# Attention scores on padded keys, a shorter way to the scale of the values, and output products that begin at the last transpose

## The chip, the cores and the metric

The kernel runs on one core of a Trainium2 chip. The metric is the device time of one execution in microseconds (us); of several runs the median is given. The profile is that of one execution.

## What is computed

The program is a chain of three layers in float32. The first is attention with rotary positions, for 4 batches, 8 heads, 576 positions and 64 features per head; two feed-forward layers follow, on 576 positions of 512 features.

```python
q_rot, k_rot = (rotate(q), rotate(k))
scores = scale * np.matmul(q_rot, k_rot.transpose(0, 1, 3, 2))
scores = scores - np.max(scores, axis=-1, keepdims=True)
attn = np.exp(scores)
attn = attn / (np.sum(attn, axis=-1, keepdims=True) + 1e-09)
return np.matmul(attn, v).astype(np.float32)
...
k = np.maximum(xk @ w_k, 0.0)
v = k * k @ w_v
r = 1.0 / (1.0 + np.exp(-(xr @ w_r)))
return (r * v).astype(np.float32)
...
h = np.maximum(xt @ w_tok1, 0.0) @ w_tok2
u = x + h.transpose(0, 2, 1)
h2 = np.maximum(u @ w_ch1, 0.0) @ w_ch2
return (u + h2).astype(np.float32)
```

## The kernel before

Every float32 product is made of three (high by high, high by low, low by high), with operands split into two parts that TensorE takes in one pass each.

Heads are worked on in 16 pairs, `g`, four for each batch. The rotated queries and keys of a pair lie in SBUF tiles of 128 rows, 64 features of the first head above 64 of the second, as a high and a low part: `spl_t[g]` holds `(kh, kl), (qh, ql)`, all of them `kq` in the rows of the profile. A pair has nine blocks of scores, `r` = 0 to 8, each of 128 query rows by 576 keys: eight are four blocks for each of the two heads, `m` the block and `x` the head, and the ninth holds the last 64 rows of both heads. `emit_S` (L366) makes a block with six matmuls into `S`, which has three PSUM buffers. A block of one head reads 64 rows of the tiles, `l`; the ninth block reads all 128, since its queries are padded with zeros. TensorE is then used in another shape: 64\*128 in the profile's rows, against 128\*128. `r` runs through the heads in turn: 0, 1, 0, 1.

VectorE takes the largest of each row (`emit_max`), ScalarE the exponentials (`emit_exp`), VectorE the reciprocals (`emit_rc`); ScalarE and VectorE make two halves in float16 (`emit_hi`, `emit_lo`). Then a transfer issued by SyncE (SP) transposes them (`emit_tr`, L415) into `pt` tiles, one for each head and each half `u` of the query rows. `emit_pv` (L426) makes the output of one half `u` of both heads, with 28 matmuls of 128\*64, the two heads in turn on the two halves of the array's columns.

The values are scaled by a power of two for each pair. `v_max` takes the largest of each row, `v_row` (L310) lays the 128 results side by side in one row by a product with the identity, `v_pow` finds the power on that row, `v_all` (L331) spreads it over 128 rows by a product with a row of ones, and `v_sc` (L337) copies it to SBUF. `v_shift` moves rows of the scaled values by transfers from SBUF to SBUF.

`a_step(j, kv)` (L492) writes the steps of all blocks; `prep(g, k)` (L453) writes the loads and the preparation of the next pairs between them. In batch 0 the weights of the second layer are prepared beside it (`Conv`). From batch 1 on, `kv` weaves the products `kp` and `vp` of the second layer, with 128\*128 matmuls, between the blocks (`kvr_gen`). The order on each engine is not that of the code alone: the framework's scheduler sorts the instructions by priorities (`PRI`, the `prio` decorators) and by times that it assumes. All transfers go through SP's one queue, in its order. The rest of the program, after 475 us, is the other two layers.

Of the kernel before, what the change touches and what calls it, by code (L numbers as in the profile page):

```python
# [8 lines left out]
F32 = mybir.dt.float32  # L9
# [9 lines left out]
NP = H // 2  # L19
# [45 lines left out]
def body(tc, kin, qin, vw, tabs, ident, mu, w_k, w_v, w_r, w_t1, w_t2, w_c1, w_c2, out):  # L65
# [41 lines left out]
    with ctx:  # L107
# [3 lines left out]
        vd = [[dram.tile([128, KD, HS], F32, name=f"vd{b}_{c}") for c in range(2)] for b in range(B)]  # L111

        idn = const.tile([128, 128], F32, name="idn")
        ones = const.tile([1, 128], F32, name="ones")
        mu_s = const.tile([128, 2, KD], F32, name="mu_s")
        om_s = const.tile([128, 2, KD], F32, name="om_s")

# [120 lines left out]
        rk_p = right("rk", BUFS["rk"])  # L238
        rq_p = right("rq", BUFS["rq"])
        tab_p = right("tab", 1)  # L240
        sp_p = right("sp", BUFS["sp"])
        vr_p = right("vr", BUFS["vr"])
        v16_p = right("v16", BUFS["v16"])
# [5 lines left out]

        tab = tab_p.tile([128, 2, QW], F32, name="tab")  # L250
        TAB = [[tab[:, k, 0:w] for k in range(2)] for w in (S, QW)]

        raw_t, v_t, v16_t, sc_t, spl_t = {}, {}, {}, {}, {}
        NG = B * NP
# [23 lines left out]
        def rope(g, j, k, e, lo=0, hi=None):  # L278
# [6 lines left out]
            if e == "P":  # L285
                last["rope"] = o

        @prio("qk")
        def split_hi(g, j, e, lo=0, hi=None):
            w = QW if j else S  # L290
            if lo == 0:
                hl = [sp_p.tile([128, w], F32R, tag=f"sp{j}{i}", name="kq") for i in range(2)]
                spl_t.setdefault(g, [None, None])[j] = hl
            hi = hi or w
            copy(e, spl_t[g][j][0][:, lo:hi], raw_t[g][j][0][:, lo:hi])

        @prio("qk")
        def split_lo(g, j, e, lo=0, hi=None):
            hi = hi or (QW if j else S)
            hl = [x[:, lo:hi] for x in spl_t[g][j]]  # L300
            tt(e, hl[1], raw_t[g][j][0][:, lo:hi], hl[0].bitcast(F32), ALU.subtract)

        @prio("v")
        def v_max(g):
            m = sm_p.tile([128, 1], F32, tag="vm", name="vm")
            dve.tensor_reduce(out=m, in_=v_t[g], op=ALU.max, axis=AX.XY, apply_absolute_value=True)
            sc_t[g] = m

        @prio("v")
        def v_row(g):  # L310
            p = pv_p.tile([128, 512], F32, tag="pv", name="vps")
            pe.matmul(p[0:1, 0:128], lhsT=sc_t[g], rhs=idn, start=True, stop=True)
            sc_t[g] = p

        @prio("v")
        def v_pow(g):

            p = sc_t[g]
            a = sm_p.tile([1, 2], F32, tag="va", name="va")
            dve.tensor_reduce(out=a[:, 0:1], in_=p[0:1, 0:128], op=ALU.max, axis=AX.X)  # L320
            dve.tensor_scalar(out=a[:, 0:1].bitcast(I32), in0=a[:, 0:1].bitcast(I32), scalar1=0x7F800000,
                              scalar2=None, op0=ALU.bitwise_and)
            r = sm_p.tile([1, 2], F32, tag="vb", name="vb")
            dve.tensor_scalar(out=a[:, 1:2], in0=a[:, 0:1], scalar1=2.0 ** -100, scalar2=2.0 ** -14,
                              op0=ALU.max, op1=ALU.mult)
            dve.tensor_scalar(out=r[:, 1:2], in0=a[:, 1:2], scalar1=1.0 / PSCALE, scalar2=None, op0=ALU.mult)
            dve.reciprocal(r[:, 0:1], a[:, 1:2])
            sc_t[g] = r

        @prio("v")  # L330
        def v_all(g):  # L331
            p = pv_p.tile([128, 512], F32, tag="pv", name="vps2")
            pe.matmul(p[:, 0:2], lhsT=ones, rhs=sc_t[g], start=True, stop=True)
            sc_t[g] = p

        @prio("v")
        def v_sc(g):  # L337
            s = sc_p.tile([128, 2], F32, tag="sc", name="sc")
            dve.tensor_copy(s, sc_t[g][:, 0:2])
            sc_t[g] = s  # L340

        @prio("v16")
        def v_hi(g):
# [18 lines left out]
        S_t, sum_t, p16_t = {}, {}, {}  # L362
        pt_t, xT = {}, {}

        @prio("S")
        def emit_S(j):  # L366
            g, r = divmod(j, ND)
            (kh, kl), (qh, ql) = spl_t[g]
            m, x = divmod(r, 2)
            l = slice(0, 128) if r == ND - 1 else slice(64 * x, 64 * x + 64)  # L370
            p = S_t[j] = S_p.tile([128, 2, 512], F32, tag="S", name="S")
            for h in range(2):
                for n, (a, b) in enumerate(((qh, kh), (qh, kl), (ql, kh))):
                    pe.matmul(p[:, h, 0:HS], lhsT=a[l, 128 * m:128 * m + 128], rhs=b[l, h * HS:(h + 1) * HS],  # L374
                              start=(n == 0), stop=(n == 2))
# [38 lines left out]
        @prio("tr")  # L414
        def emit_tr(j):  # L415
            g, r = divmod(j, ND)
            m, x = divmod(r, 2)
            t = p16_t[j].rearrange("p a b c -> p (a b c)")
            if r == ND - 1:
                for y in range(2):  # L420
                    sp.dma_start_transpose(out=pt(g, y, 1)[:, :, 256:320], in_=t[64 * y:64 * y + 64])
            else:
                sp.dma_start_transpose(out=pt(g, x, m // 2)[:, :, 128 * (m % 2):128 * (m % 2) + 128], in_=t)

        @prio("pv")
        def emit_pv(g, u):  # L426

            t0, n = UNIT[u]
            ts = [pt_t.pop((g, x, u)) for x in range(2)]
            vh, vl = v16_t[g]  # L430
            p = pv_p.tile([128, 512], F32, tag="pv", name="pv")
            prods = [(vh, j, j) for j in range(9)] + [(vl, j, j) for j in range(5)]
            for i, (v, a, c) in enumerate(prods):
                for x in range(2):
                    l = slice(64 * x, 64 * x + 64)
                    pe.matmul(p[l, 0:n], lhsT=v[:, a, l], rhs=ts[x][:, c, :], start=(i == 0),  # L436
                              stop=(i == len(prods) - 1))

            @prio("low")
            def out():  # L440
                b, pr = divmod(g, NP)
                if b not in xT:
                    xT[b] = P["xT"].tile([128, KD, S + 1], F32, tag="xT", name="xT")
                    pool.memset(xT[b][:, :, 0:1], 0.0)
                copy("D", xT[b][:, pr, 1 + t0:1 + t0 + n], p[:, 0:n], sc_t[g][:, 1:2])
                if u == 1:
                    sp.dma_start(xd[b][:, pr], xT[b][:, pr])
                    a_done.add(g)
            return out
# [3 lines left out]
        def prep(g, k):  # L453
# [12 lines left out]
                split_hi(g, 0, "A")  # L466
                v_pow(g)
            elif k == 1:
                v_all(g)
                v_sc(g)  # L470
                ld_raw(g + 1, 0, 0)
                ld_raw(g + 1, 0, 1)
            elif k == 2:
# [5 lines left out]
            elif k == 4:  # L479
                split_hi(g, 1, "A")  # L480
                split_lo(g, 1, "D")
                v_hi(g)
            elif k == 5:
                v_lo(g)
                v_shift(g)
            elif k == 6:
                v_max(g + 1) if g + 1 < NG else None

        NTT = NG * ND
        after = {}  # L490
# [174 lines left out]


        n0 = UNIT[0][1]
        usual, PRI["ld"] = PRI["ld"], 0
        ld_raw(0, 0, 0)
        sp.dma_start(tab[:, 0], tabs[:, 0])  # L670
# [10 lines left out]
        for j in range(2):  # L681
            for k in range(2):
                ld_raw(1, j, k)
        pool.memset(ones, 1.0)
        cv = Conv(lambda: P["xs"].tile([128, 2 * HS], I32, tag="xs", name="cv"),
                  wk + wv, "conv0", "rope", "P", lambda: acc_p.tile([128, 512], I32, tag="acc", name="cvp"))
        for j in range(2):
# [13 lines left out]
        v_max(0)  # L701
        v_row(0)
        v_pow(0)
        v_all(0)
        v_sc(0)
        v_hi(0)
        v_lo(0)
        v_shift(0)
# [298 lines left out]
```

## Time and profile before

| | us |
|---|---|
| median of 3 runs | 1004.59 (1001.96 to 1006.24) |
| profiled execution, span from the first to the last instruction | 997.5 |
| TensorE (PE) busy in that span | 900.2 |
| its weight loads (PEld) | 822.1 |
| VectorE (DVE) | 584.9 |
| ScalarE (ACT) | 483.7 |
| GpSimd (POOL) | 429.9 |

No other time is listed for the profiled execution than its span; what lies around the span is therefore taken from the median of the runs, 7.1 us above it. Shares of busy time are means over stages that differ: the transfer engines are busy half of the span, and nearly all of that falls into the first half. The matmuls' ends are modelled and overlap, so the distance from one start to the next tells more of TensorE's pace than their durations do. "issue" is a wait for nothing that the profile shows.

### The profile page before, as it was taken

To read this page: it belongs to the slowest core of one execution; us is meant where nothing else is said; L and a number is where in the kernel's file an instruction comes from. 1 tells how busy PE (TensorE), PEld (TensorE's weight loads), DVE (VectorE), ACT (ScalarE), POOL (GpSimd) and SP (SyncE) were. 2 spreads that over 40 slices of the span, in tenths; PEclk is the share of its full clock that TensorE was granted. 3 is DMA by queue.
4 is the path that set the end of the run, shared out by engine and by line. 5 is a ranking of instruction groups with operands and counts; after the bars stand their busy time and mean duration, and the time that the engine had idled before them with its cause. 6 is when DMAs were issued, how large, how long until landed. Compare 5 with 4: busy or idle time off the path is not lost.

```text
span 997.5 us, 17692 instructions
## 1 busy us (share of the span) xinstructions
PE 900.2 (90%) x6544; PEld 822.1 (82%) x6544; DVE 584.9 (59%) x1280; ACT 483.7 (48%) x1077; POOL 429.9 (43%) x445
## 2 busy tenths in 40 slices
PE   2654698999999889999799989999999999999997
PEld 2534466888887778888689979999999999999997
DVE  7989977767777677776897599532133211332111
ACT  3556666767677677675564565421143112211110
POOL 6257967777768765351675522410141013101010
PEclk9966658999999999999999999999999999999999
DMA  5999979898899977786920372110211001000000
GB/s 183 247 259 268 198 145 201 175 189 175 181 175 189 190 149 145 130 160 143 326 94 25 123 290 82 32 42 1 72 37 37 1 25 55 1 24 24 1 25 25
DMA packets 212343, 120.81 MB, mean 121 GB/s; under 512 B 175264, under 2 KB 193312, under 8 KB 212128
## 3 DMA queue, kind: packets, MB, share of 16 engines
q1 hardware_dynamic: 212256, 119.67, 50.9%
q8 instruction: 52, 0.85, 0.3%
q14 instruction: 35, 0.29, 0.1%
HBM read 60.90 MB, written 14.16 MB: 75 GB/s over the span
## 4 chain that ended last, share of the span: by engine, by line
PE 54%; DVE 6%; DMA 2%; POOL 2%; ACT 1%; issue 1%; SPq 0%; DVEq 0%; ACTq 0%; POOLq 0%
PE c1p L545 5%; PE co L545 5%; PE c1p L546 5%; PE c1p L547 5%; PE co L546 5%; PE co L547 5%; PE S L374 3%; PE pv L436 2%; PE rp L545 2%; PE rp L546 2%; PE rp L547 2%; PE vp L545 2%; PE vp L546 1%; PE kp L545 1%; PE vp L547 1%
## 5 line engine op out<-in xcount | busy, mean ns | idle before, releaser
L374 PE MATMUL S<-kq 64*128 64x288 f32 (+1 forms) x864 | 159.8, 342 | 32.2 <-DVE p L406 15.1
L374 PEld LDWEIGHTS S<-kq 64*128 64x128 f32 (+1 forms) x864 | 127.3, 214 | 59.2 <-issue 18.9
L387 ACT ACTIVATE S<-S,nm 128x576 f32<-128x576 f32 x144 | 102.2, 713 | 77.9 <-DVE nm L380 77.3
L906 DVE SCALAR_TENSOR_TENSOR hs<-c1p,hs 128x288 fp32r<-128x288 f32 x96 | 43.6, 454 | 158.0 <-ACT hs L905 157.9
L380 DVE TENSOR_REDUCE nm<-S 128x1 f32<-128x576 f32 x144 | 106.7, 750 | 43.0 <-PE S L374 42.6
L905 ACT ACTIVATE hs<-c1p 128x288 fp32r<-128x288 f32 x96 | 38.9, 409 | 183.8 <-PE c1p L547 180.3
L406 DVE SCALAR_TENSOR_TENSOR p<-S,rc,p 128x576 f16<-128x576 f32 x144 | 114.6, 810 | 16.7 <-ACT p L75 16.1
L104 POOL TENSOR_TENSOR uhl<-y,uhl 128x288 fp32r<-128x288 f32 x32 | 25.4, 822 | 223.9 <-ACT uhl L73 223.9
L545 PE MATMUL c1p<-uhl,parts 128*128 128x288 f32 x384 | 115.0, 300 | 3.6 <-DVE y L104 3.6
L546 PE MATMUL c1p<-uhl,parts 128*128 128x288 f32 x384 | 114.3, 298 | 0.0
L547 PE MATMUL c1p<-uhl,parts 128*128 128x288 f32 x384 | 114.2, 298 | 0.0
L75 ACT ACTIVATE p<-S,rc 128x576 f16<-128x576 f32 x144 | 104.9, 750 | 18.1 <-ACT S L387 7.4
L546 PE MATMUL co<-hs,parts 128*128 128x288 f32 x384 | 112.7, 296 | 0.0
L547 PE MATMUL co<-hs,parts 128*128 128x288 f32 x384 | 112.7, 296 | 0.0
L545 PE MATMUL co<-hs,parts 128*128 128x288 f32 x384 | 108.4, 297 | 0.0
L545 PE MATMUL kp<-xs,parts 128*128 128x288 f32 x256 | 80.9, 323 | 8.6 <-ACT t L614 5.5
L436 PE MATMUL pv<-pt,vh 128*64 128x256 f16 (+1 forms) x576 | 60.8, 328 | 29.8 <-DMA pt<-p 22.6
L545 PE MATMUL vp<-k,parts 128*128 128x288 f32 x256 | 78.7, 310 | 2.3 <-ACT vt L73 1.6
L104 POOL TENSOR_TENSOR q<-t 128x288 f32<-128x288 f32 x64 | 47.8, 749 | 72.9 <-ACT t L614 67.2
L546 PE MATMUL kp<-xs,parts 128*128 128x288 f32 x256 | 77.0, 302 | 0.1
L546 PE MATMUL vp<-k,parts 128*128 128x288 f32 x256 | 77.0, 302 | 0.0
L545 PEld LDWEIGHTS c1p<-uhl,parts 128*128 128x128 f32 x384 | 73.1, 190 | 4.5 <-POOL uhl L104 3.8
(119 smaller groups left out, 2363.1 us busy)
## 6 DMA issues: line engine op xcount, KB each, us to landing
words<-in_w_c_dram SPq DMA_DIRECT2D x24, 512.0 KB, 6.8
rq<-in_qin_dram SPq DMA_DIRECT2D x30, 320.0 KB, 3.6
rk<-in_kin_dram SPq DMA_DIRECT2D x32, 288.0 KB, 3.5
vr<-in_vw_dram SPq DMA_DIRECT2D x16, 320.0 KB, 3.6
xd<-xT SPq DMA_DIRECT2D x16, 288.5 KB, 2.7
vd<-vt SPq DMA_DIRECT2D x32, 144.0 KB, 2.4
y<-vd SPq DMA_DIRECT2D x8, 576.0 KB, 5.5
out_dram<-y SPq DMA_DIRECT2D x8, 576.0 KB, 3.6
```

The lines of the kernel that those rows point to most:

```text
L75: act.activation(out=o, in_=i, func=AF.Copy, scale=scale)
L104: return (pool if e == "P" else dve).tensor_tensor(o, a, b, op=op)
L374: pe.matmul(p[:, h, 0:HS], lhsT=a[l, 128 * m:128 * m + 128], rhs=b[l, h * HS:(h + 1) * HS], start=(n == 0), stop=(n == 2))
L380: dve.tensor_reduce(out=nm, in_=S_t[j][:, :, 0:HS], op=ALU.max, axis=AX.XY, negate=True)
L387: act.activation(out=e, in_=e, func=AF.Exp, bias=sum_t[j], accum_out=s)
L406: dve.scalar_tensor_tensor(out=t[:, 1], in0=S_t.pop(j)[:, :, 0:HS], scalar=sum_t[j], in1=t[:, 0], op0=ALU.mult, op1=ALU.subtract)
L436: pe.matmul(p[l, 0:n], lhsT=v[:, a, l], rhs=ts[x][:, c, :], start=(i == 0), stop=(i == len(prods) - 1))
L545: pe.matmul(p, lhsT=wh, rhs=t[:, 0], start=first, stop=False)
L546: pe.matmul(p, lhsT=wh, rhs=t[:, 1], start=False, stop=False)
L547: pe.matmul(p, lhsT=wl, rhs=t[:, 0], start=False, stop=last)
L905: act.activation(out=h[:, 0], in_=p[:, 0:HS], func=AF.Relu)
L906: dve.scalar_tensor_tensor(out=h[:, 1], in0=p[:, 0:HS], scalar=0.0, in1=h[:, 0].bitcast(F32), op0=ALU.max, op1=ALU.subtract)
```

## The change

Three things change. For batches 1 to 3 the keys of each head are copied by transfers (`apart`, L317 in the new numbering) into tiles `kz` of 128 rows of their own, whose other 64 rows hold zeros from the start (`zeros`); a block's scores are then made with all 128 rows, of which 64 add nothing. There is one such tile for each head and each part, so that a pair's copy follows the last use by the pair before. The blocks' order by head becomes 0, 0, 1, 1 (`place`). In the output products the second head now comes first. And the first product of the values' scale takes the column of maxima, repeated 128 times, as its stationary operand, so that the row of maxima arrives on all 128 rows at once and the second product and the copy fall away.

```diff
+        kz = [[kz_p.tile([128, S], F32R, tag=f"kz{x}{i}", name="kz") for i in range(2)] for x in range(2)]
...
+        def zeros(x):
+
+            for i in range(2):
+                pool.memset(kz[x][i][64 - 64 * x:128 - 64 * x].bitcast(F32), 0.0)
...
+        @prio("qk")
+        def apart(g, x):
+
+            if g < NP:
+                return
+            l = slice(64 * x, 64 * x + 64)
+            for i in range(2):
+                sp.dma_start(kz[x][i][l].bitcast(F32), spl_t[g][0][i][l].bitcast(F32))
...
-            pe.matmul(p[0:1, 0:128], lhsT=sc_t[g], rhs=idn, start=True, stop=True)
+            pe.matmul(p[:, 0:128], lhsT=sc_t[g].broadcast_to([128, 128]), rhs=idn, start=True, stop=True)
...
-        @prio("v")
-        def v_all(g):
-            p = pv_p.tile([128, 512], F32, tag="pv", name="vps2")
-            pe.matmul(p[:, 0:2], lhsT=ones, rhs=sc_t[g], start=True, stop=True)
-            sc_t[g] = p
-
-        @prio("v")
-        def v_sc(g):
-            s = sc_p.tile([128, 2], F32, tag="sc", name="sc")
-            dve.tensor_copy(s, sc_t[g][:, 0:2])
-            sc_t[g] = s
...
+        def place(r):
+
+            return (4, 0) if r == ND - 1 else (2 * (r // 4) + r % 2, r // 2 % 2)
...
-            m, x = divmod(r, 2)
-            l = slice(0, 128) if r == ND - 1 else slice(64 * x, 64 * x + 64)
+            m, x = place(r)
+            l = slice(0, 128)
+            if r < ND - 1 and g >= NP:
+                kh, kl = kz[x]
+            elif r < ND - 1:
+                l = slice(64 * x, 64 * x + 64)
...
-                for x in range(2):
+                for x in (1, 0):
...
+                apart(g, 0)
             elif k == 6:
                 v_max(g + 1) if g + 1 < NG else None
+            elif k == 7:
+                apart(g, 1)
```

The scheduler moves instructions with it. On TensorE, around the first half's output products of the sixth pair (`g` = 5), before (`pv` are output products, `S` scores, `kp` the second layer's):

```order
L374 MATMUL S<-kq 128x288 x12
L436 LDWEIGHTS vh
L436 MATMUL pv<-pt_2014,vh 64x256
L545 MATMUL kp<-xs,parts 128x288
L546 MATMUL kp<-xs,parts 128x288
L547 MATMUL kp<-xs,parts 128x288
...
L436 LDWEIGHTS vh
L436 MATMUL pv<-pt_2075,vh 64x256
```

The same place of the changed kernel:

```order
L386 MATMUL S<-kz,kq 128x288 x6
L448 LDWEIGHTS vh
L448 MATMUL pv<-pt_2135,vh 64x256
L448 LDWEIGHTS vh
L448 MATMUL pv<-pt_2007,vh 64x256
L448 LDWEIGHTS vh
...
L558 MATMUL kp<-xs,parts 128x288
```

Before, one product stands alone ahead of twelve `kp` matmuls and the rest behind them; now all 28 stand together, and the scores read `kz`.

On SP's queue, from the fifth pair's first transposes on (`pt<-p` are transposes, `vh<-vh` the shift of the values), before:

```order
L423 DMA_TRANSPOSE pt_1605<-p_1567 128x9x128
L263 DMA rk<-in_kin_dram 128x576
L266 DMA rq<-in_qin_dram 128x640
L423 DMA_TRANSPOSE pt_1570<-p_1602 128x9x128
L423 DMA_TRANSPOSE pt_1605<-p_1623 128x9x128
L447 DMA xd_60<-xT 128x577
L359 DMA vh<-vh 64x512
L360 DMA vh<-vh 64x512
L274 DMA vr<-in_vw_dram 128x640
L423 DMA_TRANSPOSE pt_1719<-p_1674 128x9x128
L423 DMA_TRANSPOSE pt_1767<-p_1716 128x9x128
L423 DMA_TRANSPOSE pt_1719<-p_1764 128x9x128
```

The changed kernel there:

```order
L435 DMA_TRANSPOSE pt_1643<-p_1591 128x9x128
L459 DMA xd_60<-xT 128x577
L363 DMA vh<-vh 64x512
L364 DMA vh<-vh 64x512
L435 DMA_TRANSPOSE pt_1643<-p_1611 128x9x128
L317 DMA kz<-kq 64x576 x2
L276 DMA vr<-in_vw_dram 128x640
L435 DMA_TRANSPOSE pt_1708<-p_1663 128x9x128
L435 DMA_TRANSPOSE pt_1708<-p_1705 128x9x128
L435 DMA_TRANSPOSE pt_1841<-p_1755 128x9x128
L317 DMA kz<-kq 64x576 x2
```

The two copies of the first head (high and low part) now stand behind the fourth transpose of a pair, and those of the second head behind the seventh, ahead of the eighth.

## Rows read from the trace of the kernel before

**Rows 1.** Busy time by stretch: PE, PEld, DVE, ACT, POOL, clock, DMA share, GB/s.

```profile
25.00:145.00 120.00, 76.95 (x409) 60.23 (x408) 106.27 (x231) 72.46 (x144) 77.78 (x69) 0.68 0.99 231
145.00:475.00 330.00, 313.58 (x2370) 262.58 (x2368) 234.98 (x559) 231.84 (x511) 206.88 (x218) 0.98 0.85 168
```

**Rows 2.** Timeline of TensorE, 168 to 173 us: start, duration (us), instruction.

```profile
168.63 0.30 PE L547 MATMUL kp<-xs,parts 128*128 128x288 f32 x1
168.76 0.96 PE L374 MATMUL S<-kq 128*128 128x288 f32 x6
169.56 0.29 PE L545 MATMUL kp<-xs,parts 128*128 128x288 f32 x1
...
171.03 0.30 PE L547 MATMUL kp<-xs,parts 128*128 128x288 f32 x1
171.26 1.05 PE L374 MATMUL S<-kq 64*128 64x288 f32 x6
172.25 0.40 PE L545 MATMUL kp<-xs,parts 128*128 128x288 f32 x1
172.49 0.29 PE L546 MATMUL kp<-xs,parts 128*128 128x288 f32 x1
```

**Rows 3.** Waits, 150 to 475 us: who waited for whom, total, times, longest.

```profile
PEld L436 <- issue: 12.4, 59, 1.2
PEld S L374 <- issue: 12.1, 59, 1.2
...
PE pv L436 <- DMA pt<-p: 5.5, 8, 1.5
...
PE S L374 <- DVE p L406: 5.3, 6, 1.7
```

**Rows 4.** Timeline of TensorE around an early output product, 189 to 192 us.

```profile
189.53 0.30 PE L436 MATMUL pv<-pt,vh 128*64 128x256 f16 x1
189.76 0.40 PE L545 MATMUL kp<-xs,parts 128*128 128x288 f32 x1
...
191.34 0.30 PE L547 MATMUL kp<-xs,parts 128*128 128x288 f32 x1
191.57 1.17 PE L436 MATMUL pv<-pt,vh 128*64 128x256 f16 x17
```

**Rows 5.** The tile `vps` of the values' scale: durations, and what its engine waited for.

```profile
L333 PEld LDWEIGHTS vps<-vb,ones x32: 181/184/333, 20.3 to 425.3; 1*128 1x128 f32 x32
...
  DVE vb L327: 17.7, 9
```

**Rows 6.** Timeline of TensorE around scores of both heads, 300 to 303 us.

```profile
300.92 0.30 PE L547 MATMUL kp<-xs,parts 128*128 128x288 f32 x1
301.15 1.44 PE L374 MATMUL S<-kq 64*128 64x288 f32 x12
...
302.75 0.29 PE L546 MATMUL kp<-xs,parts 128*128 128x288 f32 x1
```

**Rows 7.** Transposes in 150 to 475 us; the values' shift, issue and landing.

```profile
L423 SPq DMA_TRANSPOSE pt<-p x97: 1242/1305/2971, 149.9 to 473.5; - x97
...
L359 SPq DMA_DIRECT2D vh<-vh x16: 472/487/865, 23.1 to 437.8; - x16
...
DMA to landing us min/median/max: 2.0/2.8/6.0
```

**Rows 8.** Timeline of SP and TensorE at two passages from pair to pair.

```profile
191.47 5.57 SPq L423 DMA_TRANSPOSE pt<-p  x3
...
206.73 1.06 PE L374 MATMUL S<-kq 64*128 64x288 f32 x6
...
335.98 3.78 SPq L423 DMA_TRANSPOSE pt<-p  x2
...
338.85 1.86 PE L374 MATMUL S<-kq 64*128 64x288 f32 x18
```

**Rows 9.** Timeline of GpSimd at the start, 0 to 12 us.

```profile
8.59 2.46 POOL L104 TENSOR_TENSOR rq<-rq,tab 128x384 f32<-128x384 f32 x2 [7.59 <-DMA rq<-in_qin_dram]
```

More of the change, by code (lines that the diff above doesn't have):

```diff
@@ L113, in body @@
         idn = const.tile([128, 128], F32, name="idn")
-        ones = const.tile([1, 128], F32, name="ones")
         mu_s = const.tile([128, 2, KD], F32, name="mu_s")
@@ L240, in body @@
         tab_p = right("tab", 1)
+        kz_p = right("kz", 1)
         sp_p = right("sp", BUFS["sp"])
@@ L318, in v_pow @@
             p = sc_t[g]
-            a = sm_p.tile([1, 2], F32, tag="va", name="va")
-            dve.tensor_reduce(out=a[:, 0:1], in_=p[0:1, 0:128], op=ALU.max, axis=AX.X)
+            a = sm_p.tile([128, 2], F32, tag="va", name="va")
+            dve.tensor_reduce(out=a[:, 0:1], in_=p[:, 0:128], op=ALU.max, axis=AX.X)
             dve.tensor_scalar(out=a[:, 0:1].bitcast(I32), in0=a[:, 0:1].bitcast(I32), scalar1=0x7F800000,
                               scalar2=None, op0=ALU.bitwise_and)
-            r = sm_p.tile([1, 2], F32, tag="vb", name="vb")
+            r = sc_p.tile([128, 2], F32, tag="sc", name="sc")
             dve.tensor_scalar(out=a[:, 1:2], in0=a[:, 0:1], scalar1=2.0 ** -100, scalar2=2.0 ** -14,
                               op0=ALU.max, op1=ALU.mult)
+            dve.reciprocal(r[:, 0:1], a[:, 1:2])
             dve.tensor_scalar(out=r[:, 1:2], in0=a[:, 1:2], scalar1=1.0 / PSCALE, scalar2=None, op0=ALU.mult)
-            dve.reciprocal(r[:, 0:1], a[:, 1:2])
             sc_t[g] = r
-        @prio("v")
-        def v_all(g):
-            p = pv_p.tile([128, 512], F32, tag="pv", name="vps2")
-            pe.matmul(p[:, 0:2], lhsT=ones, rhs=sc_t[g], start=True, stop=True)
-            sc_t[g] = p
-        @prio("v")
-        def v_sc(g):
-            s = sc_p.tile([128, 2], F32, tag="sc", name="sc")
-            dve.tensor_copy(s, sc_t[g][:, 0:2])
-            sc_t[g] = s
         @prio("v16")
@@ L416, in emit_tr @@
             g, r = divmod(j, ND)
-            m, x = divmod(r, 2)
+            m, x = place(r)
             t = p16_t[j].rearrange("p a b c -> p (a b c)")
@@ L468, in prep @@
             elif k == 1:
-                v_all(g)
-                v_sc(g)
                 ld_raw(g + 1, 0, 0)
@@ L667, in body @@
         n0 = UNIT[0][1]
+        zeros(0)
+        zeros(1)
         usual, PRI["ld"] = PRI["ld"], 0
@@ L683, in body @@
                 ld_raw(1, j, k)
-        pool.memset(ones, 1.0)
         cv = Conv(lambda: P["xs"].tile([128, 2 * HS], I32, tag="xs", name="cv"),
@@ L703, in body @@
         v_pow(0)
-        v_all(0)
-        v_sc(0)
         v_hi(0)
@@ L959 @@
     lay = {}
-    z = _np.zeros((B, NP, D, 64), f32)
     def features(x, h):
@@ L965, in features @@
         return x, _np.concatenate([x[..., D // 2:, :], x[..., :D // 2, :]], axis=-2)
+    z = _np.zeros((B, NP, D, 64), f32)
     def last_apart(x, z, h):
```

## Prediction

> **What bounds the kernel now.** I read the busy time by stretch first, then TensorE's timeline, then the waits, then the queue that issues the transfers. [Rows 1] shows batch 0 of the attention (25 to 145 us) and batches 1 to 3, into which the key and value products of the next layer are woven (145 to 475); the change touches nothing behind them. In batch 0 TensorE is busy 77 of 120 us and VectorE 106: a saving on TensorE is worth little there. In batches 1 to 3 it is the other way round: TensorE 313.6 of 330 us, VectorE 235, ScalarE 232, GpSimd 207. The granted clock is 0.98 there, the 2.4 GHz level nearly throughout, so the clock has nothing to give.
>
> "Busy" hides what that time is made of, since matmuls overlap in it, so I went by their starts. [Rows 2] has both cases within 5 us. The ninth block of a pair of heads uses all 128 rows already: it starts 0.13 us behind a `kp` matmul, its six matmuls take 0.80 us (168.76 to 169.56), and `kp` goes on. A block on 64 rows starts 0.23 us behind its `kp`, takes 0.99 us (171.26 to 172.25), and the second `kp` behind it comes 0.24 us after the first instead of 0.13. That is 0.10 + 0.19 + 0.11 = 0.40 us lost by a block that stands alone, for two changes of the array's shape: 0.20 us each. The waits say it from the other side: the weight loads of scores and of output products stand 12.1 and 12.4 us, 59 times each, behind "issue", that is, behind nothing that the profile shows [rows 3].
>
> **The change part by part.** (a) Shape changes, counted in the order of TensorE's rows from the first scores of batch 1 to the last scores of all. Entries from another shape into a score, `kp` or `vp` matmul: 173 before, 38 after. Into an output product: 65 and 38. The padding takes away those between scores and `kp`/`vp`. The head order of the blocks and `(1, 0)` in the output products take away others: a product is no longer placed early with the rest behind other work (82 runs of output products over the program before, 49 after). [Rows 4] shows such a one: a single product at 189.53, `kp` from 189.76, the other products from 191.57. 135 entries by 0.20 are -27 us. Into an output product only the first interval is longer (191.34 to 191.57, 0.23 against 0.13), so 27 by 0.10 are -2.7 us.
>
> (b) The scale of the values. For each pair of heads the second product, two passes, goes, with its change of shape; the first becomes a full one, so that its change goes too. 10 pairs in the stretch: 20 passes by 0.13 and 20 entries by 0.10 are -4.6 us. Against it, the stationary operand of the first has now 128 columns; a load of 128 columns takes 0.184 us [rows 5], at most 20 by 0.184 = +3.7 us if nothing covers it. Running matmuls cover nearly all loads here; I take -4. Ahead of the second product TensorE also waits for VectorE's reciprocal, 17.7 us in 9 places over the whole program [rows 5], most of it in batch 0. In this stretch I take -2, between 0 and -4.
>
> (c) Packing lost. When blocks of both heads stand next to each other, their matmuls alternate between the halves of the array and run at once: in [rows 6] twelve of them, with what surrounds them, go from 300.92 to 302.75, 1.83 us, of which 0.40 are the two changes counted in (a). On the full array the same fourteen intervals are 14 by 0.1325 = 1.86. Each such pair gives back 1.86 - 1.43 = 0.43 us. I count 13 in the stretch (rows of twelve scores like this one): +5.6 us. So TensorE's own work is 27 + 2.7 + 4 - 5.6 = 28 us shorter.
>
> The Trainium skill, page "TensorEngine Tiling (Array Packing)", section Theoretical Speedup, speaks against the padding: up to two times for a contraction of at most 64 rows, since the tiles of the array work independently. By that rule the 96 padded blocks, 0.80 us each when full, could at best be 38 us shorter on 64 rows. The same page, Key Properties, says that a change of tiling mode drains the engine; with both rules at work, this trace shows the drain far more often than the packing, 13 pairs of a possible 48.
>
> (d) Copies of the keys: 48 transfers from SBUF to SBUF, 64 rows of 2304 B, on the queue that also issues the transposes. The nearest row is the shift of the values, 64 rows of 1024 B: 0.49 us to issue, 2.8 to land; at the worst 6.0 [rows 7]. So 24 us more on a queue that issues 97 large transposes of 1.3 us in this stretch. It runs beside TensorE until something is late. The first head's copy stands behind the fourth transpose of a pair, some four blocks ahead of its use. The second's stands behind the seventh, and is used in the third block of the next pair. [Rows 8] has a usual place and the tightest. Usual: the seventh transpose is issued by 197.04, those scores start at 206.73; 1.0 for two issues and 2.8 to land fit well into 9.7. Tightest: the seventh and eighth transposes go out from 335.98 to 339.76 and the three blocks of scores run from 338.85 to 340.64; a copy behind the seventh, at about 337.9, lands at 341.7, and TensorE would stand 1.5 us, with `kp` matmuls queued behind the scores; the transposes behind a copy are 1 us later for the output products. Bounds: nothing, to 24 sets late by 2 us, 48. I take +2. The cover is that distance; gone, each set costs what it is late.
>
> (e) The zeros: four memsets of 64x576 on GpSimd, which stands idle 7.59 us at the start until its first load lands [rows 9]. Its tensor operations of 128x384 there take 1.23 us, by columns 1.85 for 576: at most 7.4 us in all. Hidden; without that cover it would cost what it takes.
>
> (f) What the other engines give back. With 28 us less the stretch is 302 us, VectorE at 78% of it. TensorE will meet unfinished work more often: it waits 5.5 us for transposes and 5.3 for VectorE's last reading of a score buffer now [rows 3]. Bounds 0 and all 28; as the waits are small against 330 us I stay near the lower, a fifth: +6.
>
> Sum: -28 - 2 + 2 + 6 = -22 us. What follows the attention moves forward unchanged. The profiled execution's span is 997.5 us, which gives 975.5; the median of the runs is 7.1 above it, so 1004.6 - 22 = 983 us.
>
> **The rivals.** *All of it and more*: the waits don't grow, 28 + 4 = 32 us, and batch 0 gains some: 970. For it, the small waits of [rows 3]; against it, VectorE's 78%.
>
> *Another engine sets the pace*: TensorE is shorter and waits as much longer, for VectorE or for transposes in a fuller queue: 1000 to 1004. For it, the transfer engines' share of 0.85 [rows 1]; against it, no other engine is over 71% now.
>
> *The copies are late*: TensorE stands ahead of the scores in most pairs. It decides from 28/24 = 1.2 us per set on; 2 us each are 48 - 28 = 20 us slower, 1025. For it, the tight place of [rows 8]; against it, the usual one.
>
> *Packing weighs more*: if most neighbouring blocks ran packed before, the padding would lose up to 48 by 0.43 = 21 us and (a) and (b) would save half, 15: 1010. Against it, my count of 13. It is the rule of the page named above that would act there.
>
> That the change does nothing is excluded: the entries are gone from the order.
>
> **How the numbers follow.** The forecast 0.70, all and more 0.08, another engine 0.13, late copies 0.06, packing 0.03. Under 0.5% (5 us) a measurement of this kernel can hardly tell from no change. Faster: 0.70 + 0.08 + 0.03 of "another engine", 0.81; the rest of that is the same, 0.10; slower the last two, 0.09. The range goes from a little beyond "all and more" (968) into "another engine" (1002); outside are the late copies, the packing, and about half of each end, under 0.2. The likeliest alone is 973 to 993.
>
> **What would show it.** After: scores that read `kz` are 128\*128, six in 0.80 us with 0.13 on both sides; the 12.1 us of "issue" ahead of scores fall to what stands behind output products; batches 1 to 3 take about 308 us; copies land ahead of their scores. The prediction is wrong if scores wait for `kz` transfers by more than some us in all, if TensorE's idle time in the stretch, 16 us of 330 now, passes 30, or if batch 0 becomes longer.

## The result and the profile after

The changed kernel takes 994.1 us (median of four runs, 989.4 to 995.4), the kernel before 1003.3 beside it (999.4 to 1006.2): a ratio of 0.990, interval 0.9855 to 0.9944. So it is faster, by some 9 us and not by 22; 994 lies in the range, near the end that "another engine sets the pace" gave. The profiled execution of before was one of 999.4 us, its fastest; that of after took 994.6. The two spans differ by 4.7 us for that reason, and the medians decide on sizes below. So only 1.9 of the 7.1 us that the forecast put around the span lie there; the forecast change of -22 us does not depend on it.

Busy time by stretch, kernel after (PE, PEld, DVE, ACT, POOL, clock, DMA share, GB/s):

```profile
25.00:145.00 120.00, 70.75 (x407) 59.19 (x405) 107.80 (x230) 72.22 (x146) 76.91 (x68) 0.74 0.98 230
145.00:475.00 330.00, 292.13 (x2352) 268.60 (x2353) 240.27 (x555) 233.20 (x518) 209.79 (x221) 0.97 0.96 195
```

Against [rows 1], TensorE is busy 21 us less in batches 1 to 3 at the same clock, no other engine is much fuller, and the transfer engines' share has risen from 0.85 to 0.96. But the stretch is as long as it was: from the first row maximum of batch 1 to the last of all, 145.2 to 468.7 us, 323.5 us against 325.6 (147.2 to 472.8). By the forecast it would have become 22 us shorter, roughly 304 us (308 of the 330 of [rows 1]).

The padded scores do what was expected of them. TensorE's timeline around one block, kernel after (start, duration, instruction):

```profile
243.60 0.29 PE L560 MATMUL kp<-xs,parts 128*128 128x288 f32 x1
243.73 0.95 PE L386 MATMUL S<-kz,kq 128*128 128x288 f32 x6
244.51 0.33 PE L558 MATMUL kp<-xs,parts 128*128 128x288 f32 x1
244.69 0.29 PE L559 MATMUL kp<-xs,parts 128*128 128x288 f32 x1
```

Six matmuls from 243.73 to 244.51, 0.13 us behind the `kp` before them, as the ninth block in [rows 2]. What has become longer are the waits. Kernel after, TensorE's waits from 150 to 470 us and its weight loads' from 150 to 475 (total, times, longest):

```profile
PE pv L448 <- DMA pt<-p: 14.9, 14, 2.4
PE S L386 <- DVE p L418: 5.2, 5, 2.6
PE kp L558 <- ACT t L627: 4.1, 4, 2.1
PE vp L558 <- ACT t L627: 4.1, 3, 1.6
```
```profile
PEld L448 <- issue: 15.4, 37, 2.3
PEld S L386 <- issue: 12.4, 23, 2.8
```

Output products wait 14.9 us for transposes instead of 5.5 [rows 3], and `kp` and `vp` wait 8.2 for ScalarE to empty their one accumulator, a wait of 0.7 before. The wait of the scores for a free `S` buffer is what it was, 5.2 us against 5.3. The weight loads of the scores stand behind "issue" 23 times instead of 59, but each time longer: 12.4 us against 12.1.

The copies and the zeros, kernel after (durations in ns, first and last start):

```profile
L317 SPq DMA_DIRECT2D kz<-kq x48: 462/554/1678, 113.9 to 440.8; - x48
L293 POOL MEMSET kz<- x4: 571/572/573, 0.7 to 2.4; 64x576 f32 x4
```

An account of TensorE from the first score matmul of batch 1 to the last matmul of the program says where the time went. I worked it out from the starts: of each distance between two starts, 0.133 us (the pace of a 288-column matmul) is own work (between output products up to 0.17); behind a change of shape up to 0.10 us of the first and 0.11 of the second distance is the change's; the rest is wait.

| kernel | own work | shape changes (number) | waits | sum |
|---|---|---|---|---|
| before | 746.9 | 41.6 (280) | 57.5 | 846.0 |
| after | 746.9 | 12.2 (96) | 85.6 | 844.7 |
| e1, without copies | 747.4 | 13.0 (104) | 75.3 | 835.7 |
| e2, scores on 64 rows | 746.1 | 34.1 (221) | 66.3 | 846.5 |
| e13, before with two passes | 722.6 | 38.3 (263) | 79.5 | 840.4 |
| e14, after with two passes | 721.9 | 12.4 (102) | 103.4 | 837.7 |
| e18, e1 with two passes | 721.1 | 10.0 (80) | 99.8 | 830.9 |

Each row is of one execution. TensorE's own time with its shape changes fell by 29.4 us, and its waits rose by 28.1. The question for the experiments is what it now waits for.

### The profile page after: what moved, and what is told of

The parts are those of the page before. It is cut to its first block, busy times and chain, and to the rows that moved or that the text cites. A ratio compares the mean times of both kernels' runs of the same rounds, so it can differ in the third digit from the quotient of the medians.

```text
span 992.8 us, 17719 instructions
## 1 busy us (share of the span) xinstructions
PE 869.5 (88%) x6512; PEld 825.4 (83%) x6512; DVE 587.5 (59%) x1264; ACT 481.6 (49%) x1077; POOL 421.4 (42%) x448
## 4 chain that ended last, share of the span: by engine, by line
PE 49%; DVE 7%; DMA 2%; issue 1%; ACT 1%; POOL 0%; SPq 0%; DVEq 0%; ACTq 0%
PE c1p L558 5%; PE c1p L559 5%; PE c1p L560 5%; PE co L558 5%; PE co L559 5%; PE co L560 5%; PE rp L558 2%; PE rp L559 2%; PE rp L560 2%; PE S L386 1%; DVE cv L199 1%; DVE cv L202 1%; DVE cv L195 1%; DVE parts L104 1%; PE vp L559 1%
## 5 line engine op out<-in xcount | busy, mean ns | idle before, releaser
L399 ACT ACTIVATE S<-S,nm 128x576 f32<-128x576 f32 x144 | 102.5, 714 | 76.0 <-DVE nm L392 75.3
L386 PE MATMUL S<-kz,kq 128*128 128x288 f32 x576 | 96.7, 309 | 9.2 <-DVE p L418 5.2
L386 PE MATMUL S<-kq 64*128 64x288 f32 (+1 forms) x288 | 62.8, 389 | 43.6 <-DVE p L418 22.0
L386 PEld LDWEIGHTS S<-kz,kq 128*128 128x128 f32 x576 | 83.4, 195 | 16.4 <-issue 11.5
L386 PEld LDWEIGHTS S<-kq 64*128 64x128 f32 (+1 forms) x288 | 52.3, 257 | 52.4 <-issue 33.5
L558 PE MATMUL kp<-xs,parts 128*128 128x288 f32 x256 | 77.2, 309 | 13.2 <-ACT t L627 10.0
L448 PE MATMUL pv<-pt,vh 128*64 128x256 f16 (+1 forms) x576 | 51.0, 327 | 35.8 <-DMA pt<-p 31.8
L558 PE MATMUL vp<-k,parts 128*128 128x288 f32 x256 | 76.7, 302 | 4.4 <-ACT t L627 4.1
L559 PE MATMUL kp<-xs,parts 128*128 128x288 f32 x256 | 76.5, 300 | 3.4 <-POOL xs L104 3.2
```

Of the source, the lines that this page charges most:

```text
L399: act.activation(out=e, in_=e, func=AF.Exp, bias=sum_t[j], accum_out=s)
L558: pe.matmul(p, lhsT=wh, rhs=t[:, 0], start=first, stop=False)
L559: pe.matmul(p, lhsT=wh, rhs=t[:, 1], start=False, stop=False)
```

## The experiments

Theory A: the copies, and the fuller queue and transfer engines, took what TensorE gained. Theory B: the chain of a block's softmax on VectorE and ScalarE set the pace in many blocks already, so that time taken from TensorE turns into waits, with or without copies.

**e1 to e4: the parts of the change.** In e1 a padded block reads the pair's own tile on 128 rows, so that all of the shapes are as after, without copies or zeros (the scores add up both heads). e2 goes back to 64 rows and has no copies; e4 is e2 with the 48 copies made and not read; e3 has the old order of blocks and products.

```diff
 # e1
-            if r < ND - 1 and g >= NP:
-                kh, kl = kz[x]
-            elif r < ND - 1:
+            if r < ND - 1 and g < NP:
...
-                apart(g, 0)
...
 # e2, and e4 with apart kept
-            if r < ND - 1 and g >= NP:
-                kh, kl = kz[x]
-            elif r < ND - 1:
+            if r < ND - 1:
...
 # e3
-            return (4, 0) if r == ND - 1 else (2 * (r // 4) + r % 2, r // 2 % 2)
+            return divmod(r, 2)
...
-                for x in (1, 0):
+                for x in range(2):
```

> The change without its 48 copies and zeros: the scores of batches 1 to 3 read all 128 rows of the pair's own keys (so the scores are sums over both heads, another result). Theory A (the copies on the queue make transposes and output products late, and that ate the gain): what was forecast comes back, 0.975 to 0.98 of the time before, and TensorE's waits for transposes fall from 15 us to about 6. Theory B (the softmax chain on VectorE and ScalarE paces many blocks, and TensorE now waits for it): as the changed kernel, 0.985 to 0.993, waits for transposes still over 10 us.

> The change without padding: scores on 64 rows as before, no copies; the new block order, the new order of output products and the new scale of the values stay. Entries from another shape 156 into matmuls and 41 into output products (before 173 and 65). Theory A: this is 5 to 8 us faster than before, 0.992 to 0.995, and adding padding without copies (the run beside it) gives the rest. Theory B: the same 0.992 to 0.998, and the padding gives little more with or without copies.

> The change with the old block order (heads in turn) and the old order of output products, so with padding, copies and the new scale. Entries from another shape: 62 into matmuls and 62 into output products (the change: 38 and 38). TensorE's own work is 24 by 0.2 + 24 by 0.1 = 7 us more than the change's. Theory A: 0.995 to 1.000. Theory B: 0.988 to 0.994, since 7 us of TensorE's work are swallowed by waits.

> Scores on 64 rows as in the run without padding, but the 48 copies are made, and nothing reads them: the cost of the copies by itself. Theory A: 10 to 15 us slower than the run without them. Theory B: within 4 us of it.

Measured, as ratios to the kernel before: e1 0.982 (0.978 to 0.986), e2 0.995 (0.992 to 0.997), e3 0.995 (0.993 to 0.998), e4 0.9995 (0.997 to 1.002). So 48 copies cost 4.5 us where nobody reads them (e4 against e2), and about 8 us in the changed kernel (0.990 against e1). The padding alone brings 13 us (e1 against e2), the orders about 5 (0.990 against e3, where the intervals overlap). The new scale of the values is tried by itself in no run. No theory had its way: e1 lies between the two ranges, e4 a little above the 4 us of B, e3 at the lower end of A. The copies show in the transfer engines. Busy time from batch 1's first maximum to the last of all, columns as above, kernel before, after, e2, e4:

```profile
147.00:473.00 326.00, 310.14 (x2352) 260.28 (x2351) 232.91 (x552) 228.59 (x505) 205.66 (x217) 0.98 0.85 168
```
```profile
145.00:469.00 324.00, 288.95 (x2333) 265.89 (x2334) 234.27 (x543) 228.90 (x508) 206.95 (x218) 0.97 0.96 195
```
```profile
145.00:480.00 335.00, 311.08 (x2363) 270.63 (x2363) 247.03 (x558) 234.83 (x519) 213.60 (x223) 0.96 0.83 170
```
```profile
145.00:485.00 340.00, 316.56 (x2350) 270.81 (x2351) 245.95 (x557) 234.10 (x515) 214.06 (x221) 0.95 0.91 186
```

326 by 0.85 is 277 us of transfer work before, 324 by 0.96 is 311 after; e2 to e4 is 278 to 309. The copies are some 32 us of the 16 engines' work together, 0.65 each. They show on SyncE's queue too, which issues for 259 us of the stretch after instead of 220 before. Which of the two makes their price, these runs do not separate. TensorE's waits in e1, 145 to 470 us:

```profile
PE pv L446 <- DMA pt<-p: 9.6, 10, 1.4
PE S L384 <- DVE p L416: 7.7, 8, 2.4
PE kp L553 <- ACT t L622: 2.5, 6, 0.9
```

Without copies the output products wait 9.6 us for transposes, between the 5.5 of before and the 14.9 of after, and the products of the second layer 3.5 for their accumulator (2.5 here and 1.0 of `vp`) instead of 8.2. So a part of the longer waits is the copies' doing. Theory A has a share of 5 to 8 us in the missing 13; without copies e1 turns 28 us of TensorE's own time into 18 to 20 us of the whole (by the ratio and by the medians).

**e5 and e6: VectorE relieved.** The low half of the probabilities is written on 32 of 576 columns, in both kernels.

```diff
-            t = p16_t[j] = p16_p.tile([128, 2, 2, HS], F16, tag="p16", name="p16")
+            t = p16_t[j] = P16[j % 4]
...
-            dve.scalar_tensor_tensor(out=t[:, 1], in0=S_t.pop(j)[:, :, 0:HS], scalar=sum_t[j], in1=t[:, 0],
-                                     op0=ALU.mult, op1=ALU.subtract)
+            dve.scalar_tensor_tensor(out=t[:, 1, :, 0:16], in0=S_t.pop(j)[:, :, 0:16], scalar=sum_t[j],
+                                     in1=t[:, 0, :, 0:16], op0=ALU.mult, op1=ALU.subtract)
```

> The kernel before, with VectorE's share of the softmax made thin: the low half of the probabilities is written on 2x16 columns instead of 2x288 (the rest of it is zeros from the start, in four fixed buffers; the output loses that part). 109 operations of 0.81 us in batches 1 to 3 shrink to about 0.15 each, so VectorE has about 70 us less there. Batch 0, where VectorE is busy 106 of 120 us, becomes shorter in any case, by up to 20 us. Theory B (the chain max, exponential, low half paces many blocks): batches 1 to 3 become shorter by little here, since TensorE's own work of 297 us is then the bound; about 975 us. Theory A (copies and fuller transfer queue ate the gain): the same here, 975 to 985. The run serves for the difference to the changed kernel with the same cut.

> The changed kernel with the same cut as e5. Theory B: with VectorE out of the way the stretch follows TensorE again, so that most of the 30 us that TensorE's own work has become shorter shows: 20 to 28 us faster than e5. Theory A: the copies and the transposes on SP's queue remain as they are, and the difference to e5 stays what it was between the two kernels, 9 to 10 us.

Measured: e5 991.0 us, ratio 0.990 (0.985 to 0.995); e6 989.2, 0.987 (0.983 to 0.991). The gap between the kernels shrank to 2 us instead of growing to 20 or more: VectorE alone is not what TensorE waits for, and theory B in this form fell. The 9 to 10 us of theory A did not come either. The stretch of e6 shows what it met instead, a transfer share of 1.01:

```profile
138.00:430.00 292.00, 265.23 (x2177) 240.34 (x2176) 176.44 (x542) 218.07 (x485) 198.38 (x203) 0.99 1.01 209
```

**e7 and e8: even work.** The second layer's products come 2, 1 and 1 groups at a time instead of 2, 2 and 2.

```diff
-                    kv(KVN)
+                    kv(3 * n)
```

> The changed kernel with the second layer's key and value products spread evenly: 2, 1 and 1 groups of four matmuls in the three places of a block instead of 2, 2 and 2, so that they last for 32 of a batch's 36 blocks instead of 21. Theory B: pairs of heads with few kp and vp matmuls (70 to 80, 24 to 27 us) are paced by the softmax and those with 105 (31.5 us) by TensorE; evened out, the chain covers TensorE everywhere and a stretch of about 108 blocks by 2.7 us = 292 to 305 us results: 10 to 25 us faster than the changed kernel. Theory A: no gain, within 4 us of it. A third possibility: products that come late in a batch push the next layer's start back, slower.

> The kernel before with the same even spread as e7. Theory B: TensorE's work is 30 us more here, so it paces nearly every block once the work is even: a gain of 0 to 8 us on the kernel before, less than that of e7. Theory A: as e7, none.

Measured: e7 999.9, ratio 0.998 (0.995 to 1.000); e8 1003.9, 0.999 (0.996 to 1.002). No gain before, and some 6 us worse after, the third possibility: uneven work is not the cause.

**e9 to e12: the whole softmax, or the transposes.** e9 and e10 write both halves on 32 columns; e11 and e12 transpose 5 of the 9 parts of each block, and the output products read these five in place of the rest.

```diff
 # e9, e10, beside the lines of e5
-            copy("A", t[:, 0], S_t[j][:, :, 0:HS], sum_t[j])
+            copy("A", t[:, 0, :, 0:16], S_t[j][:, :, 0:16], sum_t[j])
...
 # e11, e12
-                sp.dma_start_transpose(out=pt(g, x, m // 2)[:, :, 128 * (m % 2):128 * (m % 2) + 128], in_=t)
+                sp.dma_start_transpose(out=pt(g, x, m // 2)[:, 0:5, 128 * (m % 2):128 * (m % 2) + 128], in_=t[:, 0:640])
...
-                    pe.matmul(p[l, 0:n], lhsT=v[:, a, l], rhs=ts[x][:, c, :], start=(i == 0),
+                    pe.matmul(p[l, 0:n], lhsT=v[:, a, l], rhs=ts[x][:, c % 5, :], start=(i == 0),
```

> The kernel before with both halves of the probabilities thin: ScalarE writes 2x16 columns of the high half and VectorE 2x16 of the low (the rest is zeros from the start; the output is no attention any more). e5 and e6 have told that VectorE alone isn't what paces: with it relieved the two kernels were 991.0 and 989.2. Theory B2 (ScalarE and VectorE together, the chain of a block): the light pairs fall to TensorE's pace; here, where TensorE's own work is 297 us, 960 to 985 in all. Theory A2 (the queue that issues the transposes, 0.79 to 0.93 of the time issuing in e6, and the transfer engines at 0.99 there): no gain over e5, 985 to 992.

> The changed kernel with the cut of e9. Theory B2: 20 to 28 us faster than e9, since TensorE's 30 us show once no other engine paces the blocks. Theory A2: the transfers of the changed kernel are those of before and 48 more, and they pace: 0 to 5 us of difference to e9, or slower than it.

> The kernel before with short transposes: 640 of the 1152 columns of each block of probabilities are transposed, 5 of 9 parts, and the output products read these in place of the other four (another output; as many products as before). The transposes' time on the queue and on the transfer engines falls to 5/9, about 0.6 us less for each of 97 in batches 1 to 3. Theory A2: little, 995 to 1003, since TensorE's own work bounds this kernel. Theory B2: 998 to 1004.

> The changed kernel with the cut of e11. Theory A2: the queue and the transfer engines get the room that the copies took and more; the difference to e11 grows from 9 to 10 us to 18 to 25, so about 975 to 982. Theory B2: the difference stays at about 10 us.

Measured: e9 986.7, ratio 0.985 (0.981 to 0.989); e10 976.2, 0.974 (0.971 to 0.977); e11 992.5, 0.989 (0.986 to 0.993); e12 983.3, 0.980 (0.978 to 0.983). Either relief makes both kernels faster, and leaves 11 and 9 us between them, what there was. For e10 that is neither theory's forecast, for e12 it is that of B2, and e11 is faster than both had it. Much of the relief falls into batch 0: batch 1 begins at 128.8, 132.9, 140.5 and 141.4 us (before 147.2, after 145.2). From there to the end of the span the changed kernel takes 847.6 us, e6 845.7, e12 841.5 and e10 837.9. The kernel before takes 850.3, e5 858.1, e9 852.7 and e11 850.3. These are single executions, and that of the kernel before was 4 us under its median; with that added, the reliefs bring the kernel before at most 4 us from batch 1 on, and the changed kernel 2 to 10. So the changed kernel waits for these resources more than the kernel before, and neither the softmax nor the transfers are alone the reason. In e10 the transfers step in, as in e6; its stretch, and its waits from 150 to 440 us:

```profile
133.00:434.00 301.00, 277.54 (x2244) 251.66 (x2243) 172.42 (x540) 180.44 (x497) 211.77 (x221) 0.98 1.04 210
```
```profile
PE S L388 <- DMA kz<-kq: 7.5, 11, 2.7
PE pv L450 <- DMA pt<-p: 5.9, 5, 3.1
PE kp L560 <- ACT t L629: 3.6, 6, 0.8
```

Here scores do wait for the copies, 11 times, which hardly happens in the changed kernel. In e12 the transfers, at 0.69, are hardly what holds the stretch; what does, this run does not show:

```profile
141.00:455.00 314.00, 285.18 (x2308) 257.47 (x2308) 232.84 (x537) 225.18 (x501) 205.94 (x217) 0.99 0.69 150
```

**e13 to e15, e18: what a microsecond of TensorE is worth.** The product of the queries' high part with the keys' low part is left out: four matmuls for a block instead of six, no change of shapes or transfers. e13 does so in the kernel before, e14 in the changed one, e15 in e10 and e18 in e1.

```diff
-                for n, (a, b) in enumerate(((qh, kh), (qh, kl), (ql, kh))):
+                for n, (a, b) in enumerate(((qh, kh), (ql, kh))):
```

> The kernel before with two passes for each block of scores instead of three (the product of the queries' high part with the keys' low part is left out, so the output loses that part). TensorE has 2 by 0.1325 us less for each of 108 blocks in batches 1 to 3, 26 to 29 us, and 10 us less in batch 0, where VectorE sets the pace. Theory B2 (the chain of ScalarE and VectorE paces part of the blocks already in this kernel): 8 to 15 us faster. If TensorE sets the pace here: 22 to 29.

> The changed kernel with the same cut, 28.6 us less for TensorE in batches 1 to 3. Theory B2: TensorE is no longer what paces most of the blocks, so that little of it shows: 0 to 8 us faster than the changed kernel. Theory A2 (what the change lost, it lost to its copies; TensorE still sets the pace): 20 us or more.

> The changed kernel with the thin softmax of e10 and the two passes of e14 together. Theory B2: with ScalarE and VectorE relieved TensorE sets the pace, and 15 to 28 of the 28.6 us show against e10. If the queue of the transposes, 0.77 to 0.98 of the time issuing in e10, is the pace there: under 8.

> The version without copies of e1 (its padded scores read both heads' rows, so its output is another) with two passes for each block of scores, 28.6 us less for TensorE in batches 1 to 3. If the copies are what makes TensorE's time cheap in the changed kernel: 10 to 14 us faster than e1, as e13 against the kernel before. If the softmax's pace is, without them too: 0 to 7 us faster than e1.

Measured: e13 990.5, ratio 0.986 (0.982 to 0.990), 13 us under the kernel before; e14 988.0, 0.984 (0.980 to 0.988), 6 us under the changed one; e15 966.5, 0.961 (0.957 to 0.965), 10 to 12 us under e10 (by medians, by ratios and spans); e18 978.4, 0.975 (0.972 to 0.978), 7 us under e1. The account above has TensorE's own time with shape changes down by 28 us in e13, 25 in e14, 29 in e18. A part of the gain falls into batch 0, since batch 1 begins 2.4, 0.1 and 1.3 us earlier in the profiles. Less that, of one microsecond taken from TensorE about 0.4 arrive in the kernel before, 0.25 in the changed one and 0.2 without copies. The sums of the table give 0.2, 0.3 and 0.2. That it is far from one is shown, the order of the three is not. Nor is it one price for a kernel: shape changes taken away without copies (e1) brought 18 to 20 us for 28, and no run here says why. The waits of e14, 150 to 470 us, show where the rest goes:

```profile
PE pv L448 <- DMA pt<-p: 22.8, 18, 3.0
PE kp L558 <- ACT t L627: 8.9, 10, 2.2
PE S L386 <- DVE p L418: 4.0, 5, 1.8
```

The wait for transposes is that of the changed kernel, longer (22.8 us against 14.9): TensorE does its part of a block sooner and then stands before the output product, whose transposes come at the end of the chain. e13 and e14 came out as theory B2 says, and e18 says that it holds without copies too. e15 doesn't carry it: of the 12 us between the spans 8.7 are gained in batch 0 (batch 1 begins at 124.2 us instead of 132.9) and 3 behind it, under a transfer share of 1.02.

```profile
124.00:434.00 310.00, 261.53 (x2112) 237.36 (x2113) 172.40 (x547) 183.22 (x510) 220.19 (x231) 0.97 1.02 210
```

**e16 and e17: cheaper copies.** e16 issues them from ScalarE's queue. In e17 GpSimd writes the keys' low parts straight into padded tiles, which leaves 24 copies.

```diff
 # e16
-                sp.dma_start(kz[x][i][l].bitcast(F32), spl_t[g][0][i][l].bitcast(F32))
+                act.dma_start(kz[x][i][l].bitcast(F32), spl_t[g][0][i][l].bitcast(F32))
...
 # e17
+            if j == 0:
+                for x in range(2):
+                    l = slice(64 * x, 64 * x + 64)
+                    tt(e, kzl[g % 2][x][l, lo:hi], raw_t[g][0][0][l, lo:hi],
+                       spl_t[g][0][0][l, lo:hi].bitcast(F32), ALU.subtract)
+                return
...
+            low = [(qh, kzl[g % 2][y]) for y in ((0, 1) if r == ND - 1 else (x,))]
+            prods = [(qh, kh)] + low + [(ql, kh)]
```

> The changed kernel with the 48 copies of the keys issued by ScalarE's queue instead of SyncE's. SyncE's queue has 26 us less to issue in batches 1 to 3 and the transposes don't stand behind copies; the transfer engines move the same. If the price of the copies (5 to 8 us) is the queue's: 4 to 8 us faster than the changed kernel, less what the issue costs ScalarE, which paces many blocks itself. If it is the transfer engines' (0.96 busy): the same or slower.

> The changed kernel with 24 copies instead of 48: GpSimd writes the low parts of the keys straight into padded tiles, two operations on 64 rows instead of one on 128 (about 1.7 us more for each of 12 pairs on an engine that is busy 63% of batches 1 to 3), and the ninth block multiplies both low tiles, two more passes for each pair (3 us of TensorE). All of the computation is kept. If the copies' price goes by their number (5 to 8 us for 48): 1 to 4 us faster than the changed kernel. If GpSimd's lateness counts, since the evictions of the products wait for it: the same or slower.

Measured: e16 1017.1, ratio 1.014 (1.010 to 1.018), some 24 us slower than the changed kernel; e17 996.3, 0.992 (0.989 to 0.996), which can't be told from it. In e16 each copy must wait until the last scores of the pair before have read its tile, and ScalarE, which issues in order, waits with it: some 18 us of idle time ahead of the copies, in 13 gaps, and 0.48 us for each of the 48, on an engine that the chain passes twice in every block. The output products pay for it (waits in 145 to 475 us):

```profile
PE pv L448 <- DMA pt<-p: 25.0, 15, 4.2
PE S L386 <- DVE p L418: 7.3, 10, 1.8
```

SyncE has no part in the chain but to issue. e17 doesn't settle the price of a copy: GpSimd's additional work and the two additional passes of the ninth block are in it too. The fastest kernel that computes all is the changed one.

## Why the prediction was right in direction and wrong in size

(a) to (c), TensorE's own time: forecast 28 us shorter, 29 by the account. The count of entries held, and so did the price of 0.20 us: over the whole stretch of the kernel before, the first distance behind a change from 64\*128 to 128\*128 is 0.22 us in the median and the second 0.24, against 0.13. The packing that is lost was not measured by itself. Own work is the same in both kernels, though the passes of the second product of the scale (2.6 us) are gone, so it is some 3 us by the account instead of 5.6. The padding alone is a gain of 13 us.

(b) The wait ahead of the second product is gone with it. In 145 to 470 us of the kernel before it was 1.7 us, near the 2 that were taken (1.3 of it is put down to another operation of VectorE):

```profile
PE vps L333 <- DVE den L394: 1.3, 1, 1.3
PE vps L333 <- DVE vb L327: 0.4, 1, 0.4
```

(e) The zeros: four memsets of 0.57 us at 0.7 to 2.4 us of the program, hidden, and cheaper than the bound.

**Two steps failed, (d) and (f): of the 12 us that are missing, (d) has about 6 and (f) 4 to 6.** e1 tells them apart. Without the copies the other terms, -28 - 2 + 6, had said 24 us; 18 to 20 came. With the copies it is 9, so that they cost about 8 instead of 2.

(d) The copies: forecast +2 for sets that come late. They are not late: the scores of the changed kernel wait for `kz` only once, 0.3 us. The step asked when a copy lands; it noted that the transposes behind a copy come later, and put no term of its own on that. Even where nobody reads them they cost 4.5 us (e4), and with them TensorE waits 14.9 us for transposes instead of 9.6. The work of the transfer engines, 32 us more on the 277 that they had in this stretch, is 309, more than the roughly 304 us to which the stretch was to shrink. The share of 0.85 in [rows 1] was taken as an argument for a rival only, and no work of a copy was added to it. It is a warning and no wall, since e6 with the same copies got through its stretch in 292 us, at 1.01. SyncE's queue, of which the step counted 24 us, became fuller as well, so that the transfer engines as the cause are argued, not shown: e16 and e17 were to tell, and each changed something else too.

(f) What the other engines give back: it took the small waits, 16 us of 330, as a sign that TensorE sets the pace, and took a fifth, 6 of 28 us. Without copies they gave back 8 to 10 (e1), and with the copies' price on top 20 of 29. The premise was wrong in the kernel before already: of 28 us taken from TensorE by e13, 13 arrived. TensorE looked full because it filled its time between the links of the chain with shape changes and with `kp` and `vp`; when the shape changes went, the same blocks ended at the same time, and the gaps became waits for transposes and for the accumulator. e1 has the same stretch, 323 us, with 30 more `kp` matmuls done in it. The Trainium skill, page "Perfetto Trace Analysis", section Identifying the Most-Contended Engine, says that the busy share of matmuls is no good measure of how close a kernel is to its roofline, and names the busy share of weight loads beside the share of peak arithmetic instead. The trace agrees on the first: the matmuls were busy 0.95 of the time [rows 1], and less than half of e13's cut arrived. Whether the weight loads, 0.80 before [rows 1] and 0.81 after, would have told it, no run here shows.

Which links of the chain hold the changed kernel is narrowed, not settled. From batch 1 on VectorE alone brings about nothing (e6: 2 us by the spans, -3 by the medians less the gain of batch 0), ScalarE with it 6 to 10 (e10) and the shorter transposes 6 to 7 (e12). That several resources hold it in turn is what these runs are consistent with; a kernel with the thin softmax and the short transposes together, or the thin softmax without copies, would show it, and was not tried. With every edit the scheduler also sorts the instructions anew, so that no run is its edit alone.

Of the rivals, "another engine sets the pace" was nearest in mechanism, without a single engine; late copies and packing did not happen. Of the signs named, idle time passed 30 us (38 of 330), the stretch did not shrink to 308, and the "issue" ahead of the scores did not fall: it was no measure of the shape changes. The gain lies within the range because the range took in a rival, not because the sum held.

## What to carry to other kernels

A busy share of 0.95 says that an engine has no idle time, not that its time counts. Before pricing what can be saved on it, find out what a known cut there is worth, and sum up the work of every other resource in the stretch, transfer engines and queues included, against the length that the stretch is to have: a saving that goes below one of these sums should not be counted on. A transfer has two prices, its own delay and the room that it takes from other transfers, and a copy that lands in time still pays the second. And a transfer that must wait for a buffer belongs on a queue whose engine is not in the chain.

## What the hardware showed beside

A wait leaves part of the price of a shape change: behind a stop TensorE's second distance is longer without any change of shape. Timeline of the kernel after:

```profile
286.12 0.29 PE L560 MATMUL kp<-xs,parts 128*128 128x288 f32 x1
286.25 0.94 PE L386 MATMUL S<-kz,kq 128*128 128x288 f32 x6
287.37 0.40 PE L558 MATMUL kp<-xs,parts 128*128 128x288 f32 x1 [0.17 <-ACT t L627]
287.61 0.29 PE L559 MATMUL kp<-xs,parts 128*128 128x288 f32 x1
287.73 0.29 PE L560 MATMUL kp<-xs,parts 128*128 128x288 f32 x1
```

The `kp` at 287.37 waited for ScalarE, and the next starts 0.24 us behind it instead of 0.13, as behind the 64-row block in [rows 2]. Batches 1 to 3 have 28 such stops between 128\*128 matmuls (a distance over 0.35 us), with 0.24 us behind them in the median. So a shape change that turns into a wait gives back less than it cost. And the transfer engines' share reached 1.04 (e10): the times of its packets overlap, so that a share of 0.96 is a sign of pressure and no measure of what is left. The same section of the Trainium skill calls the share of the 16 engines misleading, and the 1.04 agrees.
